# A linear-attention block with an MLP on one core: key sums in three groups, value weights loaded twice, a new order of the work ahead of the MLP

## The chip, the core and the metric

The kernel runs on one core of a Trainium2 chip. The core has five engines that work side by side, each through its own list of instructions in order: TensorE (PE, with its weight loads shown as PEld), VectorE (DVE), ScalarE (ACT), GpSimd (POOL) and SyncE (SP), which here only issues DMA transfers. Engines wait for each other through semaphores. The metric is the device time of one execution in microseconds (us).

## The reference

The input x has 2048 rows of 576 bf16 numbers. There are 32 heads of 18 numbers. Layer norms have no learned scale.

```
y        = layernorm(x)
q, k, v  = y @ wqkv                                  (each 2048 x 576, in 32 heads)
phi(t)   = [softmax(t @ w_phi), softmax(-t @ w_phi)]  per head, 36 features
kv, z    = sum over all rows of phi(k) v^T  and of phi(k)
o        = phi(q) kv / (phi(q) z + 1e-6)
h        = x + o @ wo
out      = h + gelu(layernorm(h) @ w1 + b1) @ w2 + b2  (hidden width 4608)
```

No query can be finished before the sums kv and z over all 2048 rows are there.

## The kernel before, in words

Rows are held in 16 tiles of 128, taken as eight pairs p = 0..7 with two tiles a = 0, 1 each; 576 columns are two halves i = 0, 1 of 288. All engines run a list that is written out by hand: the calls from line 771 on are the program order, and each engine takes its own instructions from it in that order.

Every function named here issues instructions for one engine (or the queue of one):

- Setup: `load_wk`, `load_x`, `load_values`, `load_wq`, `load_wo`, `load_w1`, `load_biases` are DMA issues on SP's queue (some slices of w1 on POOL's). `warm` runs products of an identity matrix on TensorE. `spread` (L217, POOL) lays w_phi out as blocks `bd`.
- Folding: `flip_mm` (L365) transposes the key weights on TensorE, `flip_ev` (L371) copies the result out, `fold_k_mm` (L381) multiplies them by the blocks, so that one product gives k @ w_phi; `fold_k_ev` (L389) copies to `wkp`. The query weights are turned by DMA (`turn_wq`, L374), folded by `fold_mm("q", c)` (L396), and `swap_q` copies row halves between partitions.
- Layer norm: `stats` (L293, L294, DVE), `power` (L300, L302, POOL: a variance to the power -1/2), `centre` (L266, POOL), `scale` (L272 on ACT or L314 on DVE). Then the tile is transposed: for pairs 0 and 1 on TensorE (`turn_x_mm`, `turn_x_ev`), for the others by DMA (`turn_dma`, L321).
- Projections: `key_mm`, `value_mm`, `query_mm` (all L426). A projection is 18 products of 64 rows each, for a = 0 on partitions 0-63 and a = 1 on 64-127, 288 columns wide. Weights must therefore stand in both halves of the partitions: `load_values` fills partitions 0-63 of `wv`, and `copy_values` (L174, POOL) copies to 64-127.
- After a projection: `key_exp`, `query_exp` (L448, ACT, two exponentials), `value_ev` (L436, ACT); `key_sum` (L477, L479, DVE) gives reciprocal sums; `key_weigh` (L483) multiplies by them, on POOL.
- `sums(p, a)` (L562): 11 products of full height (128 rows) that add one tile's phi(k) v^T to `acc_kv`. They need both halves i of the weighed features of that tile.
- The turn to the MLP: `table` (DVE) masks the sums, `combine_mm` (L648) multiplies the queries of tiles 0 and 1 by them, `divide` (L661, L662, DVE), `turn_o_mm`, `residual_mm` (L697), `residual_add` (L706), `residual_stats` (L714), `second` (L719, L254 and a root on POOL, L256), `rescale` (L260), `turn2_mm`, `turn2_ev` (L343). Query projections stand between these steps.
- The MLP: `up` (L1150, L1172) and `down` (L1194, L1198) for one, one, two, two, two pairs; the attention of later pairs (`norm_q`, `leave`, `enter`) is called from inside these loops.

PSUM results of the part ahead of the MLP rotate through three buffers (`two`, bufs=3), so a product waits until the result three steps before it has been copied out. Weighed keys rotate through five buffers (`exk_pool`). The weights of the first half of the setup borrow the memory of `w1_0`, and wkp, the turned queries of pair 0 and the MLP's input share `shared`.

## Time and profile before

| | us |
|---|---|
| median of 3 runs | 392.02 (391.94 to 392.32) |
| the profiled execution | 392.69 |
| its span, first to last instruction | 391.0 |
| first key projection starts | 15.82 |
| first combination of queries with the sums | 71.03 |
| MLP starts | 85.23 |
| first `down` starts | 103.15 |

The profile names engines as above, with the line of the kernel; "pk", "pv", "pW", "acc_kv", "pn", "pa", "ph" and "po" are the PSUM tiles of key and query projections, value projections, folds, key sums, combinations, residual, and the MLP's two products. In a row of the timeline or chain stand the start, the length and the number of instructions. The end of a product is modelled, so a product that waits in the pipeline can count as busy.

### The profile page before, as it was taken

Reading aid. Unit: us, or ns where it says so; the run is one execution under the profiler, and the core shown is the slowest. Engines: PE = TensorE matmul, PEld = TensorE weight load, DVE = VectorE, ACT = ScalarE, POOL = GpSimd, SP = SyncE. Lnnn points to the kernel's source line nnn. Section 1 sums busy time; section 2 is a strip of 40 time slices with the busy share of each in tenths; the row PEclk is TensorE's granted clock in tenths of the full one; section 3 lists DMA queues with packets and bytes.
Section 4 is the critical chain, followed back from the end, with each engine's and each line's share of the span. In section 5 each row is a group of like instructions: output and inputs, shape, how many; then the busy total and the mean of one; then the engine's idle time right before and its main releaser. Section 6 shows DMA issues by size and latency. Waiting matters only on the chain.

```text
span 391.0 us, 10251 instructions
## 1 busy us (share of the span) xinstructions
PE 383.6 (98%) x4492; PEld 267.2 (68%) x4493; DVE 163.5 (42%) x367; ACT 163.7 (42%) x290; POOL 128.2 (33%) x167
## 2 busy tenths in 40 slices
PE   8899999999999999999999999999999999999997
PEld 4687777779878887844457887444677764447773
DVE  6989894595249388590029322000480000000100
ACT  3978887678501850056650000666300026661000
POOL 8899999214604564144003111000031110000120
PEclk9999999999999999999999999999999999999999
DMA  8999749999655666643005542000041000000000
GB/s 220 189 182 175 163 98 184 227 300 254 206 106 104 95 107 134 107 61 62 0 2 63 90 106 48 16 1 2 2 102 50 17 17 0 2 2 0 17 29 18
DMA packets 76108, 34.76 MB, mean 89 GB/s; under 512 B 63026, under 2 KB 73536, under 8 KB 76064
## 3 DMA queue, kind: packets, MB, share of 16 engines
q1 hardware_dynamic: 75376, 32.47, 41.9%
q0 software_dynamic: 400, 1.35, 1.3%
q8 instruction: 35, 0.57, 0.6%
q10 hardware_dynamic: 288, 0.30, 0.3%
q14 instruction: 9, 0.07, 0.1%
HBM read 16.53 MB, written 2.36 MB: 48 GB/s over the span
## 4 chain that ended last, share of the span: by engine, by line
PE 94%; DVE 4%; POOL 1%; issue 1%; POOLq 0%
PE po L1194 36%; PE ph L1150 36%; PE pk L426 7%; PE pa L697 5%; PE pv L426 4%; PE acc_kv L562 2%; PE pw L250 1%; PE pn L648 1%; DVE st L293 1%; POOL wv L174 1%; DVE ob L662 0%; PE pW L396 0%; DVE shared L260 0%; PE pT L338 0%; DVE shared L314 0%
## 5 line engine op out<-in xcount | busy, mean ns | idle before, releaser
L1172 ACT ACTIVATE home<-ph,b1col 128x512 bf16<-128x512 f32 (+1 forms) x180 | 98.5, 598 | 169.6 <-PE ph L1150 166.3
L1194 PE MATMUL po<-w,home 128*128 128x288 bf16 (+2 forms) x1151 | 143.3, 286 | 0.1
L1150 PE MATMUL ph<-shared,w 64*128 64x512 bf16 (+2 forms) x1638 | 141.3, 332 | 0.1
L1194 PEld LDWEIGHTS <-home 128*128 128x128 bf16 x1152 | 109.2, 98 | 32.3 <-issue 1.8
L1150 PEld LDWEIGHTS <-w 64*128 64x128 bf16 x1638 | 80.3, 94 | 60.0 <-issue 1.0
L1198 DVE TENSOR_TENSOR ot<-po,hb 128x288 bf16<-128x288 f32 (+2 forms) x32 | 14.5, 454 | 106.5 <-PE po L1194 100.7
L1183 POOL TENSOR_TENSOR hb<-xh,b2bc 128x576 f32<-128x576 bf16 x16 | 20.4, 1272 | 104.6 <-DVE ot L1198 95.2
L426 PEld LDWEIGHTS <-home 64*128 64x128 bf16 x864 | 42.0, 94 | 10.8 <-issue 1.1
L512 POOL TENSOR_TENSOR padded<-home,rq 128x540 bf16<-128x540 bf16 x32 | 34.8, 1101 | 36.4 <-DVE rq L504 14.9
L256 POOL TENSOR_TENSOR rs<-va,mhalf 128x1 f32<-128x1 f32 x16 | 8.8, 550 | 105.0 <-DVE va L254 105.0
L706 DVE TENSOR_TENSOR xh<-pa,xh 128x288 bf16<-128x288 f32 x32 | 13.2, 449 | 71.6 <-PE pa L697 71.6
L483 POOL TENSOR_TENSOR phik<-phik,rk 128x576 bf16<-128x576 bf16 x32 | 36.4, 1164 | 1.4 <-PE pv L426 0.9
L477 DVE TENSOR_REDUCE sk<-phik 128x64 f32<-128x1152 bf16 x16 | 21.2, 1327 | 5.4 <-ACT phik L448 5.4
L448 ACT ACTIVATE home<-pk 128x576 bf16<-128x576 f32 x32 | 18.9, 649 | 6.9 <-PE pk L426 5.7
L503 DVE TENSOR_REDUCE sk<-home 128x64 f32<-128x1152 bf16 x16 | 21.0, 1313 | 0.0
L426 PE MATMUL pv<-wv,home 64*128 64x288 bf16 x288 | 20.9, 283 | 0.1
L426 PE MATMUL pk<-wqp,home 64*128 64x288 bf16 x288 | 20.0, 283 | 0.2 <-ACT home L448 0.2
L448 ACT ACTIVATE phik<-pk 128x576 bf16<-128x576 f32 x32 | 18.7, 652 | 3.1 <-PE pk L426 3.1
L426 PE MATMUL pk<-shared,home 64*128 64x288 bf16 x288 | 19.9, 283 | 0.0
L661 DVE RECIPROCAL rec<-pn 128x18 f32<-128x18 f32 (+1 forms) x32 | 8.0, 250 | 27.9 <-PE pn L648 27.9
L697 PE MATMUL pa<-wo,shared 64*128 64x288 bf16 x288 | 18.8, 283 | 0.0
L697 PEld LDWEIGHTS <-shared 64*128 64x128 bf16 x288 | 13.9, 94 | 4.3 <-issue 0.5
(78 smaller groups left out, 209.0 us busy)
## 6 DMA issues: line engine op xcount, KB each, us to landing
w<-in_B_w_dram SPq DMA_DIRECT2D x21, 432.0 KB, 7.0
out_dram<-ot SPq DMA_DIRECT2D x15, 144.0 KB, 1.9
xh<-in_A_x_dram SPq DMA_DIRECT2D x3, 576.0 KB, 7.3
wo<-in_A_wo_dram SPq DMA_DIRECT2D x4, 324.0 KB, 6.3
w<-in_B_w_dram POOLq DMA_DIRECT2D x3, 432.0 KB, 10.5
wv<-in_A_wqkv_dram SPq DMA_DIRECT2D x2, 324.0 KB, 9.9
w<-in_A_wqkv_dram SPq DMA_DIRECT2D x4, 157.5 KB, 8.7
wqp<-wqp SPq DMA_DIRECT2D x2, 288.0 KB, 3.9
```

Source lines behind the costliest of these rows:

```text
L426: nc.tensor.matmul(dst[:, a, 0:HALF], lhs[rows, c, :], w[rows, slot, i * HALF : (i + 1) * HALF], start=(n == 0), stop=(n == KC - 1),)
L448: nc.scalar.activation(rows[:, :, i * HH : (i + 1) * HH, s, :], flight[key, p, i][:, :, 0:HALF].rearrange("p a (h f) -> p a h f", f=DH), A ...
L477: nc.vector.tensor_reduce(sk[:, :, :], part_of(dst, i), AX.X, ALU.add)
L483: eng.tensor_tensor(part, part, flight["r" + key, p, i][:, a, :].rearrange("p (h o) -> p h o", o=1).to_broadcast([P, NH, DH]), ALU.mult,)
L503: nc.vector.tensor_reduce(sk[:, :, :], part_of(phiq[p], i), AX.X, ALU.add)
L512: eng.tensor_tensor(padded[:, a, g0 * P : (g0 + 5) * P].rearrange("p (g k) -> p g k", k=P)[:, :, 0:STEP].rearrange("p g (h f) -> p g h f", ...
L697: nc.tensor.matmul(pa[a], oT[p % 2][rows, c, :], wo[rows, c, cs], start=(c == 0), stop=(c == KC - 1),)
L1150: nc.tensor.matmul(ph[half][:, lo:hi], w1[p_ // 9][rows, c, p_ % 9 * P : (p_ % 9 + 1) * P], ln2T[rows, c, base + lo : base + hi], start=(c ...
L1172: nc.scalar.activation(hidden(m), ph[half][:, 0:width], AF.Gelu_apprx_tanh, bias=b1col[:, m : m + 1], scale=1.0,)
L1183: nc.gpsimd.tensor_tensor(hb[:, :], xh[:, t, :], b2bc[:, :], ALU.add)
L1194: nc.tensor.matmul(po[:, :], hidden(m)[:, i_ * P : (i_ + 1) * P], w2[m // 18][:, m % 18, cs], start=(j == 0), stop=(j == NM - 1),)
L1198: nc.vector.tensor_tensor(ot[:, cs], po[:, :], hb[:, cs], ALU.add)
```

## The change

- The key weights `wk` are loaded by row chunks (64, 256 and 256 rows of 576) and kept 640 wide with zeros; `flip_mm(c)` transposes one row chunk for all five head groups, and `flip_ev` copies 5 x 128 columns.
- The first key projection adds its nine chunks in the order in which they were folded.
- `load_values(e, half)` loads the value weights from DRAM into both halves of the partitions, in four loads of full rows; `copy_values` is gone.
- `load_wq(c)` loads one chunk per call, and the calls stand apart in the order; `load_wo(half)` takes nine rows of wo as one piece, with the columns of `divide`'s output ordered to match (runs of 2 instead of 18).
- `power(p)` serves one pair for p = 0..3, and two pairs in one call for p = 4 and 6 (the roots of 4 tiles).
- `ones` moves from POOL to DVE, the last slice of w_phi from POOL's DMA queue to ACT's, and three `key_weigh` calls from POOL to DVE. The masks of `window_masks` come later.
- `rescale(t)` writes one half of the doubled MLP input, `mirror(t, dve)` copies it to the other.
- `warm(12)` for `warm(13)`, and a new order for everything up to the MLP. The `sums` stand in three groups.

The helpers, cut:

```
-    def load_values(i):
-        nc.sync.dma_start(
-            wv[0:KH, :, i * HALF : (i + 1) * HALF],
...
-    def copy_values(i, part, copy):
-        cs = slice(i * HALF, (i + 1) * HALF)
-        ks = slice(part * 5, 5 + part * 4)
-        copy(wv[KH:P, ks, cs], wv[0:KH, ks, cs])
+    def load_values(e, half=0, eng=nc.sync):
+        c0, c1 = ((0, 5), (5, KC))[e]
+        eng.dma_start(
+            wv[half * KH : (half + 1) * KH, c0:c1, :],
+            A_wqkv[c0 * KH : c1 * KH, 2 * D : 3 * D].rearrange("(c k) f -> k c f", k=KH),
+        )
...
     def power(p):
...
+        n = 2 if p < 4 else 4
+        at = 2 * (p % 2)
+        va = small.tile([P, 4], FP32, name="va", tag="va")
+        nc.gpsimd.tensor_scalar(
+            va[:, 0:n], moments[p // 2][:, at : at + n, 1], 1.0, EPS, ALU.mult, ALU.add
+        )
+        rs = small.tile([P, 4], FP32, name="rs", tag="rs")
+        nc.gpsimd.tensor_tensor(rs[:, 0:n], va[:, 0:n], mhalf[:, 0:n], ALU.pow)
...
-    def flip_mm(g):
+    def flip_mm(c):
+        pX = flight["w", c] = two.tile([P, NG, P], BF16, name="pX", tag="two")
+        for g in range(NG):
             nc.tensor.transpose(
+                pX[:, g, :], wk[:, c, g * 126 : g * 126 + P], ident[:, :]
             )
...
-        features("k", wkp, p, i, PLAIN)
+        features("k", wkp, p, i, PLAIN if p or i else [(c, c) for c in fold_order])
...
+    def load_wo(half):
+        nc.sync.dma_start(
+            wo[half * KH : (half + 1) * KH, :, :],
+            A_wo.rearrange("(k c) f -> k c f", c=KC),
+        )
...
-                o[:, :, :, h0:h1],
-                pv[:, :, 0:DH].rearrange("p h (c e) -> p c e h", e=2),
+                o[:, :, h0:h1, :],
+                pv[:, :, 0:DH].rearrange("p h (e c) -> p c h e", e=2),
...
-    def rescale(t, half):
+    def rescale(t):
         mv, rs = moved[t]
-        normalise(ln2[t % 2][:, :, half, :], chunks(t), mv, rs, 0)
+        normalise(ln2[t % 2][:, :, 0, :], chunks(t), mv, rs, 0)
+
+    def mirror(t, copy):
+        copy(ln2[t % 2][:, :, 1, :], ln2[t % 2][:, :, 0, :])
```

The order that TensorE sees from the first key projection to the residual, before and after (k, v, q: a projection of pair and half; s: the key sums of pair and tile; f: a query fold):

```
before: k00 k01 v00 k10 v01 v11 k20 k21 v10 s00 v20 k11 v21 k30 v30 k31 s01 v31 f0 s20 s21
        f3 f2 v41 f1 k40 f4 k41 s10 s11 k50 k51 s31 v40 q00 v50 s41 s30 q01 q50 s40 v51 k60
        q30 k61 s51 v60 s50 v61 k70 k71 q70 v70 q40 s61 q71 v71 q20 s60 s70 s71 q60
        combine, q41 q31, transpose of o, q10 residual q61 residual q51 q11 q21
after:  k00 v01 v00 k10 v10 v11 k11 k01 k20 v20 k21 v21 k30 v30 v31 f1 s10 f2 s11 f3 s01 f0 f4
        s00 k31 k40 v40 k50 k51 k41 q00 v41 s20 s21 s31 s30 v51 v50 q01 q20 k60 v60 k61 q40 v70
        k70 v61 k71 q70 v71 q31 q30 q60 s50 s40 s41 s51 s61 s60 s70 s71 q50
        combine, q71 q51, transpose of o, q10 residual q41 residual q11 q21 q61
```

SP's queue up to the last turn of the query weights, before and after:

```
before: wk wk wk, x 2-3, x 4-7, values, values, x 8-11, wq (5 loads), turn of pair 2, wo, wq turn 4,
        wo, wq turn 1, turn of pair 3, wq turns 2, 3, 0, turn of pair 4, x 12-15, wo, ...
after:  wk wk wk, x 2-3, x 4-7, values (4 loads), x 8-11, wq 4, 2, 0, 1, wq turn 4, wq 3, turn of
        pair 2, x 12-15, wq turn 0, turn of pair 3, wq turns 3, 2, 1, biases, turns of pairs 4, 5, ...
```

More of the change, by code (lines that the diff above doesn't have):

```diff
@@ L585, with load_w1 @@
     w2 = []
-    def load_w1(q, n, eng):
+    def load_w1(q, n):
         c0, half = n // 2 * 3, n % 2
-        eng.dma_start(
+        (nc.gpsimd if q and half else nc.sync).dma_start(
             w1[q][half * KH : (half + 1) * KH, c0 : c0 + 3, :],
@@ L903 @@
     value_mm(3, 0)
-    key_weigh(2, 0, 0, pool)
-    value_ev(3, 0, act)
-    turn_wq(3)
-    turn_wq(0)
+    value_ev(3, 0, act)
+    key_weigh(1, 1, 0, pool)
+    key_weigh(0, 1, 1, pool)
+    value_mm(3, 1)
+    value_ev(3, 1, act)
+    key_weigh(1, 1, 1, pool)
+    fold_mm("q", 1)
+    fold_ev("q", 1, act)
+    load_biases()
+    sums(1, 0)
+    scale(5, 0, vec)
+    key_weigh(0, 1, 0, pool)
+    fold_mm("q", 2)
+    fold_ev("q", 2, act)
+    sums(1, 1)
+    key_sum(2, 0)
+    fold_mm("q", 3)
@@ L908 @@
+    sums(0, 1)
+    fold_ev("q", 3, act)
+    turn_dma(4)
+    scale(5, 1, vec)
+    key_weigh(2, 0, 1, pool)
+    turn_dma(5)
+    fold_mm("q", 0)
+    fold_ev("q", 0, act)
+    fold_mm("q", 4)
+    sums(0, 0)
+    key_sum(3, 0)
+    key_weigh(2, 0, 0, pool)
+    stats(6, 0)
+    swap_q(2)
+    key_weigh(3, 0, 1, pool)
+    key_weigh(3, 0, 0, pool)
+    fold_ev("q", 4, act)
+    swap_q(0)
+    key_sum(2, 1)
+    key_weigh(2, 1, 1, pool)
+    key_weigh(2, 1, 0, pool)
     key_mm(3, 1)
     key_exp(3, 1)
-    key_sum(1, 0)
@@ L979 @@
+    key_mm(5, 1)
+    key_exp(5, 1)
+    stats(6, 1)
     stats(7, 0)
     stats(7, 1)
-    sums(4, 1)
+    power(6)
+    centre(6, 1)
+    key_mm(4, 1)
+    centre(7, 0)
+    key_sum(4, 0)
+    swap_q(1)
+    query_mm(0, 0)
+    load_w1(0, 0)
+    value_mm(4, 1)
+    sums(2, 0)
+    load_wo(0)
+    key_exp(4, 1)
+    key_weigh(4, 0, 1, pool)
+    query_exp(0, 0)
+    scale(6, 1, act)
+    scale(6, 0, vec)
+    turn_dma(6)
+    scale(7, 0, act)
+    key_weigh(4, 0, 0, pool)
+    value_ev(4, 1, act)
@@ L1022 @@
[L1022 to L1027 removed]
+    turn_dma(7)
+    query_mm(0, 1)
+    query_mm(2, 0)
+    query_exp(0, 1)
+    query_exp(2, 0)
+    key_mm(6, 0)
+    key_exp(6, 0)
+    query_sum(0, 0)
+    query_weigh(0, 0, 0, pool)
+    value_mm(6, 0)
+    value_ev(6, 0, act)
+    key_mm(6, 1)
+    query_mm(4, 0)
+    value_mm(7, 0)
+    key_exp(6, 1)
+    query_exp(4, 0)
+    query_weigh(0, 0, 1, pool)
```

527 lines of the change are left out of this document (216 added, 311 removed).

## The prediction

> **What bounds the kernel now.** I read the busy shares first, then a table by stages, then the chain of work that ended last, and last the timeline of the head. The page's first line and five rows of the table by stages (stretch, length, busy time of PE, PEld, DVE, ACT and POOL, granted clock, DMA share, GB/s):
>
> ```profile
> PE 383.6 (98%) x4492; PEld 267.2 (68%) x4493; DVE 163.5 (42%) x367; ACT 163.7 (42%) x290; POOL 128.2 (33%) x167
> 6.94:15.82 8.88, 6.90 (x134) 5.58 (x133) 8.08 (x24) 7.84 (x14) 7.60 (x15) 1.00 1.13 234
> 15.82:20.78 4.96, 4.84 (x75) 3.79 (x74) 4.75 (x13) 4.43 (x8) 4.67 (x5) 1.00 0.96 145
> 20.78:71.03 50.25, 50.25 (x867) 39.17 (x866) 39.41 (x61) 40.51 (x69) 46.16 (x52) 1.00 0.91 164
> 71.03:85.23 14.20, 13.15 (x214) 10.15 (x212) 10.38 (x29) 10.12 (x18) 2.58 (x5) 1.00 1.05 258
> 85.23:391.00 305.77, 302.95 (x3195) 206.57 (x3196) 97.10 (x230) 99.33 (x182) 61.73 (x72) 1.00 0.30 61
> ```
>
> TensorE is the bound: from 20.78 to 71.03 it has no idle time. The MLP behind 85.23 is out of reach: the edits there touch DVE alone, which is busy 97 of 306 us. So the change can act on four things: the head before 15.82, TensorE's waits that a row counts as busy, the price of TensorE's changes between kinds of work, and the 1.05 us of idle time between 71.03 and 85.23. The chain shows the second and third:
>
> ```profile
> 16.84 1.38 POOL wv L174
> ...
> 19.35 1.39 POOL wv L174
> ...
> 20.78 2.36 PE pv L426 x35
> ...
> 25.35 1.10 PE pv L426 x18
> 26.45 0.41 PE acc_kv L562 x11
> 26.87 1.21 PE pv L426 x18
> ...
> 35.21 0.37 PE pW L396 x5
> 35.58 0.63 PE acc_kv L562 x22
> 36.21 0.54 PE pW L396 x10
> 36.74 1.21 PE pv L426 x18
> ...
> 68.84 1.04 PE acc_kv L562 x33
> 69.88 1.21 PE pk L426 x18
> ```
>
> A projection (18 products of 64 rows) costs 1.10 us, but 1.21 behind a full-height group (the key sums acc_kv or the folds pW). Eleven key-sum products cost 0.41 alone and 33 cost 1.04, so eleven more cost (1.04-0.41)/2 = 0.315. A visit to full-height work therefore costs 0.41-0.315 = 0.10 on the way in and 1.21-1.10 = 0.11 on the way out: 0.2 us, whatever it holds. Between 15.82 and 71.03 the chain has 13 such visits, the first at 26.45, the last at 68.84.
>
> **The sum for the stretch as it is.** 41 projections (16 key, 16 value, 9 query) at 1.103 are 45.2; 16 key sums at 0.315 are 5.0; five folds at 0.27 (ten products in 0.54) are 1.35; 13 visits are 2.6. That is 54.2, and the stretch has 71.03-15.82 = 55.2: 1.0 us is waiting hidden in busy rows. Part of it is seen in the head:
>
> ```profile
> 1.42 5.73 PE L250 MATMUL pw<-ident 128*128 128x512 bf16 x13 [1.42 <-POOL ident masks.py:199]
> 6.94 1.94 PE L365 MATMUL pX<-ident,w 128*128 128x128 bf16 x25
> 9.49 0.69 ACT L343 COPY home<-pT 128x640 bf16<-128x640 bf16 x1
> 10.11 5.06 ACT L389 CAST shared<-pW 128x576 bf16<-128x576 f32 x9
> 15.21 0.68 PE L338 MATMUL pT<-ident,shared 128*128 128x128 bf16 x9 [1.17 <-ACT shared L389]
> 15.82 2.38 PE L426 MATMUL pk<-shared,home 64*128 64x288 bf16 x36
> 18.04 1.50 PE L426 MATMUL pv<-wv,home 64*128 64x288 bf16 x18
> ```
>
> The value projection at 18.04 has 1.50 where two key projections have 2.38: it sits among POOL's copies of the value weights.
>
> **The change, part by part.**
>
> *Head, to the first key projection.* One warm-up product less (5.73/13 = 0.44) ends the warm-up at 6.5. The transposes of the key weights now go by row chunk and are copied 640 wide, four by ACT at 0.69, so ACT is through at 7.0+2.8 = 9.8; then the nine fold copies (5.06) and one turn copy of 0.69 before the ninth: 15.5. DVE has, from about 8.1 on (6.5 and four of five groups of transposes at 1.94/5), two copies, four tiles' statistics and four rescales to do before that; by the rows further down 0.42, 1.1 and 0.5 each, 7.4 in all, so it comes out level. So the first key projection starts at 15.5 instead of 15.82: -0.3. Bounds: the first transposes cannot start before the load (no earlier than now), 0; if the copies overlap as closely as the casts, -0.7.
>
> *POOL.* Off it go the four value copies, the ones (to DVE), three key weighings (to DVE) and two of eight root calls. TensorE gains only what waited for the copies. The ones come on DVE before the first key's reduction, and the first key sum on TensorE 15 projections (16.5 us) later, which covers them whatever they cost. A weighing on DVE costs between 0.5 (a rescale of the same elements) and 1.16 (POOL's own); I take 0.8, and three of them fit DVE's free 10.8 us between 20.78 and 71.03.
>
> *Key sums.* The new order holds them in three groups: four between the five query folds in one full-height block, four in one block after the value projection of pair 4, the last eight in one block. Three visits for 13: -10 x 0.2 = -2.0. Bounds: nothing, if TensorE waits inside the blocks for the weighings by as much; -2.1, if the folds also cost less.
>
> *Loads.* Rows for the queue (issue time, then issue to landing), the transfers' sizes from the page:
>
> ```profile
> L374 SPq DMA_TRANSPOSE w<-w x5: 1214/1253/1957, 20.0 to 28.2; - x5
> ...
> DMA to landing us min/median/max: 2.6/4.2/4.7
> L164 SPq DMA_DIRECT2D wv<-in_A_wqkv_dram x2: 705/867/1029, 3.6 to 4.4; - x2
> ...
> DMA to landing us min/median/max: 9.1/9.9/10.8
> ...
> wv<-in_A_wqkv_dram SPq DMA_DIRECT2D x2, 324.0 KB, 9.9
> ...
> xh<-in_A_x_dram SPq DMA_DIRECT2D x3, 576.0 KB, 7.3
> ...
> wo<-in_A_wo_dram SPq DMA_DIRECT2D x4, 324.0 KB, 6.3
> ```
>
> The second row half of the value weights is 648 KB more; the values landed at 4.4+10.8 = 15.2 and are now wanted at 15.5+1.1 = 16.6. The last turned piece of the query weights landed at 28.2+4.2 = 32.4, and the first query fold came at 35.21. In the new order that fold is reached after 15 projections: 15.5+16.5+0.1 = 32.1, and it takes the piece that is turned last. Before this turn stand 648 KB of values and the last 576 KB of x that came later before; 648 KB of output weights have gone behind it. [...] I take a landing at 32.5 to 33.3 and so waits of 1.2 us in all (values, pair 2's turn and this fold share them), against 1.0 before: +0.2. [...]
>
> *From the combination to the MLP.* The work is the same (seven query projections on TensorE); its end is set by DVE:
>
> ```profile
> 79.74 0.46 DVE L706 TENSOR_TENSOR xh<-pa,xh 128x288 bf16<-128x288 f32 x1 [0.40 <-PE pa L697]
> 80.23 0.46 DVE L714 BATCH_NORM_STATS2 st<-xh 128x6 f32<-128x288 bf16 x1
> 80.72 0.21 DVE L719 BATCH_NORM_AGGREGATE mv<-st 128x2 f32<-128x12 f32 x1
> 80.97 0.15 DVE L254 TENSOR_SCALAR va<-mv 128x1 f32<-128x1 f32 x1
> 82.37 2.01 DVE L260 TENSOR_SCALAR shared<-xh,mv,rs 128x576 bf16<-128x576 bf16 x4
> 84.31 1.67 DVE L343 COPY shared<-pT 128x512 bf16<-128x512 bf16 x4
> ```
>
> Two adds 0.92, two statistics 0.92, two aggregates 0.42, two variances 0.3, four rescales 2.0, two of the four copies 0.83: 5.4 of the 5.5 us from 79.74 to 85.23. Two of the rescales become copies of the same 576 elements; between nothing and 0.5 each, I take 0.4, nearer to the rescale: -0.2, and with the adds first the POOL root is covered, -0.1: -0.3 in all. The division has the same elements in runs of 2 instead of 18; I put it at nothing, with +1.8 (four of them doubled) as the far end.
>
> *All else* (roots for four tiles at once, output weights in two loads, biases earlier, a slice of the feature weights on ACT's queue) lies beside TensorE's work; the MLP's weights start when the last key sum ends and move with it.
>
> **Sum.** -0.3 -2.0 +0.2 -0.3 = -2.4 us. The profiled execution takes 392.69 (span 391.0), 0.7 above the median of 392.02; a difference made within the first holds for the second: 389.6.
>
> **The rivals.**
>
> *The weights come late (slower).* Place: the first query fold. For it: a saturated queue (DMA share 1.13 in the head), 576 KB more before the last turn, the fold 3 us earlier. [...] If the second value halves are not cheap and the 648 KB of output weights give nothing back, 1224 KB at 164 to 234 GB/s are 5.4 to 7.6 us: a landing at 37.8 to 40.0, where TensorE waits 5.7 to 7.9 us and 1.0 was waited before; with the -2.6 of the other terms 394.1 to 396.3, at the middle 395.2. It decides from a landing at 35.7 on (3.6 us of waiting). [...] Chance 0.17.
>
> *The last block waits for weighings.* POOL's weighings are the one thing that ended close before the last sums:
>
> ```profile
> 65.10 3.40 POOL L483 TENSOR_TENSOR phik<-phik,rk 128x576 bf16<-128x576 bf16 x3
> ...
> L483 POOL TENSOR_TENSOR phik<-phik,rk x32: 1159/1163/1171, 22.1 to 67.3; 128x576 bf16<-128x576 bf16 x32
> ```
>
> They end at 68.5. I have the new last one at about 65 (from 21.7 on 29 at 1.16 are 33.7, and POOL's other work in the stretch is 46.2 - 32 x 1.16 = 9.0) and the last two sums at 67 to 68. If POOL ends at 68.5 as now, the sums end at 69.1 and the combination starts at 70.4: -0.6 -0.3, 391.1. [...] No lengthening shows in the row: 32 weighings lie within 1159 and 1171 ns beside a busy DVE. Chance 0.09.
>
> *A visit is not what costs.* If what looks like the price of a change is paid in any order, only -0.3+0.2-0.3 are left: 391.6, within 0.2%. Against: 1.21 and 1.10 alternate exactly so. Chance 0.08.
>
> *More.* All waits go (-1.0 instead of +0.2) and the head gains 0.7: 392.0-0.7-2.0-1.0-0.4 = 387.9. Chance 0.12.
>
> **How the numbers follow.** The forecast, 388.4 to 391.0 around 389.6, has 0.54. Within 0.2% (0.8 us, about what the runs can tell apart) lies the fourth case's 0.08. Faster by more: 0.54, 0.12 and the 0.09, which ends just outside; slower 0.17. The range goes from 387.3, below the largest gain, to 392.8, into the late weights; this leaves out the rest of that rival and a little below, under 0.2.
>
> **What would show it.** Key sums in three groups on TensorE with 0.315 per eleven; the first key projection near 15.5; no POOL copy of wv; the first query fold without an idle line before it, or, if I am wrong, a wait of its weight load for the DMA that writes w; the combination at 69, the MLP at 82.5, and from there the same 306 us. A wait inside the last block for POOL, or a division that takes 0.9, would make the forecast wrong.

## The result: 0.9% slower, and the profile after

The changed kernel takes 395.62 us (median of five runs, 395.07 to 396.6) beside 392.13 (391.94 to 392.36) for the kernel before: a ratio of 1.0089, with a 95% interval of 1.0072 to 1.0105. The forecast was 389.6 with a range of 387.3 to 392.8. The profiled execution of the changed kernel took 396.6 (span 394.9), that of the kernel before 392.69 (391.0), so the two traces differ by 3.9.

The busy shares and the table by stages of the changed kernel (stretch, length, busy time of PE, PEld, DVE, ACT and POOL, granted clock, DMA share, GB/s). The stretches end at the first key projection, the first query fold, the last block of key sums, the combination and the MLP:

```profile
PE 381.9 (97%) x4491; PEld 265.2 (67%) x4492; DVE 169.0 (43%) x370; ACT 164.5 (42%) x292; POOL 116.6 (30%) x153
0.00:15.71 15.71, 11.12 (x146) 7.12 (x147) 10.94 (x34) 9.89 (x17) 8.47 (x29) 1.00 0.91 229
15.71:35.03 19.32, 16.99 (x273) 12.91 (x271) 16.24 (x34) 15.77 (x26) 11.18 (x16) 1.00 0.91 157
35.03:67.07 32.04, 32.04 (x566) 25.77 (x564) 30.19 (x39) 26.94 (x47) 28.89 (x31) 1.00 0.97 176
67.07:75.02 7.95, 5.40 (x109) 3.97 (x107) 5.13 (x9) 2.37 (x5) 4.66 (x5) 0.86 0.64 144
75.02:89.26 14.24, 13.41 (x215) 10.64 (x214) 9.94 (x29) 9.73 (x18) 1.51 (x3) 0.96 1.05 278
89.26:394.90 305.64, 302.95 (x3195) 204.78 (x3196) 96.52 (x230) 99.82 (x182) 61.86 (x72) 1.00 0.29 59
```

The first key projection starts 0.1 earlier than before, the 14.2 us from the combination to the MLP and the 305.6 behind it are what they were. All of the loss lies between 15.71 and 75.02: 59.3 us, where it was 55.2. TensorE is idle in both ends of this part, from 15.71 to 35.03 and from 67.07 to 75.02. The view of the waits, from 15 to 73 (engine and product, releaser, us in total, times, longest), and the chain of work that ended last say for what:

```profile
PE pk L423 <- DMA home<-shared: 2.3, 2, 1.6
PE acc_kv L559 <- POOL phik L480: 2.0, 2, 1.3
...
PE acc_kv L559 <- DVE phik L480: 0.6, 1, 0.6
```

```profile
22.08 3.26 DMA home<-shared
...
25.66 5.91 DMA home<-shared
...
60.10 5.13 DVE phik L480
65.23 1.27 DVE sk L474
...
69.18 3.10 POOL phik L480 x2
...
72.81 2.27 PE pk L423 x18
```

Three things are new. **In the head** two key projections wait for the turns of x, pair 2 (landed 22.08+3.26 = 25.35) and pair 3 (25.66+5.91 = 31.57): 0.86 and 1.8 from the end of the product before, 2.7 in all (the view counts 2.3, because the modelled end of that product reaches into the wait). **In the last block of key sums** TensorE waits for weighings, in three pieces of 0.7, 0.9 and 1.5, counted in the same way: the chain goes back from them to one weighing on DVE that took 5.1 to 5.2. **Behind that block** a query projection takes 2.27 instead of the 1.21 that it takes behind full-height work, at a granted clock of 0.50 (rows in experiment 4).

The sum over the stretch: -2.0 for the visits, -1.0 for the waits that were there before, +2.7, +3.1 and +1.1 give +3.9, against 59.3-55.2 = +4.1.

### The profile page after: what moved, and what is told of

Its sections match the earlier page's. It is cut to its first block, busy times and chain, and to the rows that moved or that the text cites. A ratio compares the mean times of both kernels' runs of the same rounds, so it can differ in the third digit from the quotient of the medians.

```text
span 394.9 us, 10223 instructions
## 1 busy us (share of the span) xinstructions
PE 381.9 (97%) x4491; PEld 265.2 (67%) x4492; DVE 169.0 (43%) x370; ACT 164.5 (42%) x292; POOL 116.6 (30%) x153
## 4 chain that ended last, share of the span: by engine, by line
PE 81%; DVE 9%; DMA 4%; POOL 2%; ACT 1%; issue 1%; POOLq 0%; DVEq 0%
PE po L1188 36%; PE ph L1144 36%; PE pa L691 5%; DVE sk L474 3%; DMA home<-shared 2%; PE pk L423 2%; DVE st L275 1%; PE pn L642 1%; DMA w<-in_A_w_phi_dram 1%; DVE phik L480 1%; DVE rk L476 1%; POOL phik L480 1%; DVE shared L310 1%; DVE sk L500 1%; POOL rs L288 1%
## 5 line engine op out<-in xcount | busy, mean ns | idle before, releaser
L1144 PEld LDWEIGHTS <-w 64*128 64x128 bf16 x1638 | 78.4, 94 | 62.1 <-issue 0.7
L480 POOL TENSOR_TENSOR phik<-phik,rk 128x576 bf16<-128x576 bf16 x29 | 33.7, 1194 | 10.5 <-DVE rk L476 10.5
L423 PE MATMUL pv<-wv,home 64*128 64x288 bf16 x288 | 19.6, 283 | 0.0
```

The lines of the kernel that those rows point to most:

```text
L423: nc.tensor.matmul(dst[:, a, 0 : hi - lo], lhs[rows, c, :], w[rows, slot, lo:hi], start=(n == 0), stop=(n == KC - 1),)
L480: eng.tensor_tensor(part, part, flight["r" + key, p, i][:, a, :].rearrange("p (h o) -> p h o", o=1).to_broadcast([P, NH, DH]), ALU.mult,)
L1144: nc.tensor.matmul(ph[half][:, lo:hi], w1[p_ // 9][rows, c, p_ % 9 * P : (p_ % 9 + 1) * P], ln2T[rows, c, base + lo : base + hi], start=(c ...
```

## The experiments

Each kernel was run beside the kernel before on the same chip; ratios are to that kernel, with 95% intervals. The changed kernel was not run again beside them; the median of the kernel before lies between 392.08 and 392.47 there, so a difference of some 0.4 us from the changed kernel says nothing. One more spread matters for single traces: the changed kernel and experiments 1 to 4 have the same head, and reach the first key projection between 15.00 and 16.27. A start later on is therefore best read from there.

**1. One weighing back to POOL.**

```
-    key_weigh(5, 1, 0, vec)
+    key_weigh(5, 1, 0, pool)
```

> One word is changed in the kernel after: the weighing of pair 5, tile 1, row half 0 goes from DVE back to POOL; the two other weighings on DVE stay. Theory A (that weighing, 5.2 us on DVE beside four weighings on POOL, made the last key sums late; the idle TensorE then lost its clock): POOL goes on without its idle 4.6 us and ends its weighings near 64.6 + 3 x 1.16 = 68.1, at most 0.5 later where one of DVE's two falls beside them; the last key sum ends near 69.2 instead of 72.8, the projection behind it takes 1.1 instead of 2.3, and the kernel 395.6 - 3.6 - 1.2 = 390.8, between 390.4 and 392. Rival B (POOL alone is the bound of the last block, whoever does that weighing): the weighing costs POOL 1.16 more and the kernel takes 395.6 or up to 396.8. Rival C (the weighing was slow by itself, by its shape or place): the two that stay on DVE are of the same shape and would be slow again where they have been 0.69 and 1.71.

Measured: 392.14 us, ratio 0.9986 [0.9971, 1.0002]; 3.5 us less than the changed kernel, for one word. The combination starts at 71.0 instead of 75.0; from the first key projection (15.00 here) it is 56.0 us instead of 59.3. The waits for weighings are gone from the list, and the projection behind the block takes 1.21. The weighings of this kernel (engine, tiles, count, shortest/median/longest in ns, first and last start):

```profile
L480 POOL TENSOR_TENSOR phik<-phik,rk x30: 1162/1166/1170, 24.4 to 66.9; 128x576 bf16<-128x576 bf16 x30
...
L480 DVE TENSOR_TENSOR phik<-phik,rk x2: 745/2266/3786, 64.9 to 68.6; 128x576 bf16<-128x576 bf16 x2
```

The same instruction takes 0.745 or 3.786 here, 0.693 to 5.215 in the changed kernel: so not its shape (rival C) but what runs beside it. And the two that stayed are still held up, only not where TensorE waits for them. Theory A holds on the cause; it had expected 390.8 and a range to 392.0, so the gain is smaller than its sum, and just outside its range.

**2. All three back to POOL.**

> In the kernel after all three weighings go from DVE back to POOL. Theory A (DVE and POOL hold each other up when both weigh): no weighing on POOL takes more than 1.17, where two took 1.46 and 1.67; POOL has five weighings left at 64.6 and ends near 64.6 + 5 x 1.165 = 70.4, the last key sum near 70.9; TensorE's wait is then about 1 us in more than one piece and the clock stays up: 395.6 - 1.9 - 1.2 = 392.5, between 391.5 and 394, which is slower than with one weighing given back. Rival B (three weighings on DVE cost nothing and POOL's total decides): slower than after by up to 3 x 1.16 = 3.5, up to 399.

Measured: 393.33 us, 1.0017 [1.0002, 1.0032]. No weighing on POOL takes more than 1.18, TensorE waits 0.7 for one, and the combination starts at 72.4 (56.2 behind the first key projection, which came at 16.27): 2.3 us faster than the changed kernel, 1.2 slower than with one given back. Rival B, by which more work on POOL could only cost, is out.

**3. What the two engines do to each other.** The timelines of the changed kernel on DVE and on POOL (start, length, engine, instruction, count, idle time before it and its releaser):

```profile
60.01 5.21 DVE L480 TENSOR_TENSOR phik<-phik,rk 128x576 bf16<-128x576 bf16 x1
65.15 1.34 DVE L474 TENSOR_REDUCE sk<-phik 128x64 f32<-128x1152 bf16 x1
...
59.81 0.32 POOL L519 TENSOR_TENSOR padded<-home,rq 128x72 bf16<-128x72 bf16 x1
60.08 4.53 POOL L480 TENSOR_TENSOR phik<-phik,rk 128x576 bf16<-128x576 bf16 x4
69.18 3.09 POOL L480 TENSOR_TENSOR phik<-phik,rk 128x576 bf16<-128x576 bf16 x2 [4.57 <-DVE rk L476]
```

DVE's weighing stands from 60.01, 0.2 after POOL began a short instruction (L519), and ends at 65.23, 0.62 after POOL's four weighings in a row have ended at 64.61. Behind it in DVE's order are the key sums of pair 7, whose factors POOL needs, so POOL then stands idle for 4.57, and TensorE for 3.1. In the weighing of experiment 1 that took 3.786 the same holds (POOL's run ends at 68.10, DVE's weighing at 68.71).

The kernel before has no such instruction on DVE beside POOL's weighings. Its costliest groups on DVE from 15 to 80 (line, engine, operation, tiles, count, busy time, mean ns, idle time before) read one tile each; the rescale takes its two factors for each row besides:

```profile
L477 DVE TENSOR_REDUCE sk<-phik 128x64 f32<-128x1152 bf16 x16 | 21.2, 1327 | 5.4 <-ACT phik L448 5.4
L479 DVE RECIPROCAL rk<-sk 128x64 f32<-128x64 f32 x16 | 8.8, 553 | 0.8
L293 DVE BATCH_NORM_STATS2 st<-xh 128x6 f32<-128x288 bf16 x18 | 7.0, 433 | 0.0
L314 DVE TENSOR_SCALAR shared<-xh,mv,rs 128x576 bf16<-128x576 bf16 x6 | 2.9, 490 | 0.0
```

To change the place of an operand, and not the work, the next kernel lets DVE read the factors from PSUM, where TensorE's results stand, instead of SBUF, where both operands of a weighing stood:

```
+    def set_apart(p, i, a):
+        n = 400 + 32 * len(apart)
+        apart[p, i, a] = acc_kv[:, 0, n : n + NH]
+        nc.vector.tensor_copy(apart[p, i, a], flight["rk", p, i][:, a, :])
...
-            flight["r" + key, p, i][:, a, :].rearrange("p (h o) -> p h o", o=1).to_broadcast(
+            apart.get((p, i, a), flight["r" + key, p, i][:, a, :]).rearrange("p (h o) -> p h o", o=1).to_broadcast(
...
     key_sum(5, 1)
+    set_apart(5, 1, 0)
...
     key_sum(7, 0)
+    set_apart(7, 0, 0)
...
+    key_sum(7, 1)
+    set_apart(7, 1, 1)
     sums(5, 0)
     sums(4, 0)
-    key_sum(7, 1)
```

> The kernel after, with its three weighings still on DVE, but each reads its 32 factors from a free part of the key sums' bank in PSUM, where DVE puts a copy of them right behind the key sum (three copies of 32 columns; the key sum of pair 7, half 1 is called for a few steps earlier, which leaves DVE's order but for the copies as it was). So each weighing has one operand in SBUF and one in PSUM. Theory A (two operands in SBUF make DVE wait for POOL's run of weighings, and POOL for DVE): no DVE weighing takes more than 1.2, none on POOL more than 1.18, POOL's idle 4.6 us behind 64.6 is gone, the last key sum ends near 69.7, the combination starts near 70.9 instead of 75.0, and the kernel takes 395.6 - 3.7 = 391.9, between 391.2 and 392.8. Rival B (DVE and POOL hold each other up wherever the factors are): a weighing of 3 to 5 us on DVE again, the kernel within 1 us of 395.6.

```profile
L487 POOL TENSOR_TENSOR phik<-phik,rk x29: 1162/1166/1171, 23.9 to 66.5; 128x576 bf16<-128x576 bf16 x29
...
L487 DVE TENSOR_TENSOR phik<-phik,acc_kv x3: 694/753/754, 60.4 to 70.6; 128x576 bf16<-128x576 bf16 x3
```

All three weighings take 0.69 to 0.75, and no weighing on POOL is lengthened. Only the first of them, at 60.44, lies beside POOL's weighings; in the last kernel below all three do (57.49, 60.36 and 63.30, 0.69 to 0.76), again without lengthening POOL's. That is theory A on the cause. The time is another matter: 394.41 us, 1.0057 [1.0038, 1.0077], where 391.9 was expected. The factors lie in the tile of the key sums, so DVE's last two weighings now wait 4.4 us for TensorE's key sums, and TensorE 1.7 for them, and the projection behind them takes 2.27 at half the clock again. The cause was removed and a dependence of my own put in its place; the last kernel below avoids it.

**4. The clock.** Nine products into a bank that nobody reads keep TensorE busy during the waits:

```
+    warm(3)
     sums(7, 0)
     key_weigh(7, 0, 1, pool)
     key_weigh(7, 1, 1, vec)
+    warm(6)
     sums(7, 1)
```

> Nine products into a bank that nobody reads are added in the kernel after: three ahead of the key sums of pair 7, tile 0, and six ahead of those of tile 1 (2 us of TensorE's 3.1 us of waiting there). The waits themselves stay. Theory A (the low granted clock at 72.7 to 76 comes from the idle TensorE just before): the last key sum ends at 72.8 as before, the projection behind it takes 1.1 to 1.3 instead of 2.3, the combination 0.7 instead of 1.1, and the kernel 395.6 - 1.5 = 394.1. Rival B (the clock falls there for another reason): the projection takes 2.3 again and the time is the same or up to 0.5 longer.

Measured: 395.37 us, 1.0064 [1.0042, 1.0087], 0.3 less than the changed kernel by the medians and 0.25% less by the ratios, whose intervals overlap: the runs do not tell the two apart. The profiled execution cannot decide either, because in it the first weighing on DVE got in and the waits are gone: the same instructions up to 60 us, but another winner.

```profile
60.23 0.72 DVE L480 TENSOR_TENSOR phik<-phik,rk 128x576 bf16<-128x576 bf16 x1
...
60.02 0.31 POOL L519 TENSOR_TENSOR padded<-home,rq 128x72 bf16<-128x72 bf16 x1
60.28 8.32 POOL L480 TENSOR_TENSOR phik<-phik,rk 128x576 bf16<-128x576 bf16 x6
```

So the outcome can differ between executions. The clock differs too, and its record in the traces shows a pattern. In the changed kernel's trace the record starts with the full clock at 4.46 us; the clock falls to half at 72.73, 20 times 3.413 us later, and stays there for 3.41. In the traces of experiments 3 and 7 and of the second kernel of experiment 10 it falls 19 times 3.413 us after the start of the record, again for 3.41. Tables in these lengths, for the changed kernel and then for experiment 5 (the turns first, below), both with more than 3 us of waiting in this block:

```profile
69.31:72.73 3.42, 1.05 (x22) 0.80 (x22) 1.94 (x2) 0.13 (x1) 2.96 (x2) 1.00 0.64 136
72.73:76.14 3.41, 3.41 (x44) 2.29 (x40) 1.16 (x5) 1.02 (x2) 1.95 (x3) 0.50 0.50 125
76.14:79.55 3.41, 3.13 (x50) 2.29 (x49) 2.50 (x9) 2.25 (x5) 0.00 (x0) 1.00 1.05 226
```

```profile
65.81:69.23 3.42, 1.87 (x60) 1.64 (x56) 3.32 (x5) 1.87 (x4) 1.19 (x1) 1.00 1.09 262
69.23:72.64 3.41, 1.79 (x35) 1.40 (x35) 1.81 (x5) 0.00 (x0) 2.24 (x3) 1.00 0.24 52
72.64:76.05 3.41, 3.27 (x62) 2.36 (x58) 2.53 (x9) 2.39 (x5) 1.61 (x3) 1.00 0.86 188
```

In the changed kernel the waits fall into one of these lengths, in which TensorE works 1.05 of 3.42, and the next is granted half the clock. In experiment 5 they lie in two of them, 1.87 and 1.79 of work are left, and the clock stays at 1.00. The other three traces with a fall have 1.20, 1.77 and 1.72 of work in the length ahead of the half clock; the third kernel of experiment 10 has 1.60 and no fall, so no limit can be read from the work in one length.

So in the four traces with a fall the low clock comes behind the waiting, as theory A has it, but waits as long were followed by none in experiment 5. That it depends on how the waits lie in these lengths is my reading, and the 1.60 speaks against it; what decides is not shown. Executions with a lower mean clock are 3 of 5 for the changed kernel and 7 of 9, 5 of 6 and 4 of 5 in experiments 5, 7 and 8, which keep these waits, and 1 of 12 in experiment 1, which does not (a mean does not say where in the run the clock fell). The two of the changed kernel that kept theirs took 395.07 and 395.25, so the clock is a small part of its loss. The kernel before has lower clocks as well: of its executions beside experiments 1, 2, 4 and 5, the 21 with a mean clock of 0.999 or more have a median of 392.28, the seven with 0.991 to 0.996 one of 393.62.

**5. The turns first.** Only SP's order is changed:

```
-    turn_wq(4)
     scale(2, 0, act)
+    turn_dma(2)
+    turn_wq(4)
...
-    turn_dma(2)
...
-    load_x(12, 16)
-    turn_wq(0)
...
     turn_dma(3)
+    turn_wq(0)
+    load_x(12, 16)
```

> Only SP's order is changed in the kernel after: the turn of pair 2 is issued ahead of the first turn of the query weights, and the turn of pair 3 ahead of the load of the last x and the second turn of the query weights. Theory A (SP works in order, so those two turns waited behind a turn that waited for its load): the turn of pair 2 lands near 21.8 as before the change, that of pair 3 near 27 to 28, TensorE's two waits of 0.86 and 1.8 for them are gone; TensorE reaches the first query fold near 32.4 instead of 35.0, and the piece of the query weights that this fold takes is turned last and still lands near 34, so 1 to 1.7 of the 2.7 come back there. With POOL, DVE and the last block as they are, the kernel takes 395.6 - 1.0 = 394.6, between 393 and 395.6. Rival B (the transfers are late because the queues are full, whatever the order): the turns land no earlier, and the time is the same within 0.5.

Measured: 395.32 us, 1.0067 [1.0045, 1.0089]. The two waits for turns are gone. In their place, as foreseen:

```profile
PE pW L393 <- DMA w<-w: 1.1, 1, 1.1
```

The waits in the last block stay (2.0 for POOL, 1.2 for DVE), which leaves 0.3 of the median, less than was expected and inside the spread of its runs (392.88 to 397.04).

**6. The value loads alone**, in the kernel before:

```
-    def load_values(i):
+    def load_values(i, half=0):
...
-            wv[0:KH, :, i * HALF : (i + 1) * HALF],
+            wv[half * KH : (half + 1) * KH, :, i * HALF : (i + 1) * HALF],
...
     load_values(0)
+    load_values(0, 1)
     load_values(1)
+    load_values(1, 1)
...
-    copy_values(0, 1, gps)
-    copy_values(1, 1, gps)
-    copy_values(0, 0, gps)
-    copy_values(1, 0, gps)
```

> The kernel before, with nothing but its value weights loaded as in the change: each of the two loads has a twin that fills rows 64 to 127, right behind it on SP, and POOL's four copies are gone. Theory A (the prediction's small term: POOL is relieved, the loads cost little): the value projections in the head no longer stand among copies, and the kernel takes 391.7 to 392.3. Rival B (648 KB more ahead of x 8 to 11 and the query weights, at 234 GB/s 2.8 us later for all that stands behind them): the values land near 18, the first value projection waits up to 1 us, the turns of pair 2 and of the query weights come later, and the kernel takes 393 to 395.

Measured: 395.42 us, 1.0073 [1.0059, 1.0088]. This part by itself costs 3.0 us. One wait and two issues on SP tell how:

```profile
PE pk L426 <- DMA home<-shared: 2.9, 1, 2.9
```

```profile
7.18 3.47 SPq L179 DMA_DIRECT2D xh<-in_A_x_dram  x1
19.42 1.44 SPq L321 DMA_TRANSPOSE home<-shared  x1
```

The queue backs up: the issue of x 8 to 11 behind the values takes 3.47 where it took 1.1 before. The turn of pair 2 is issued at 19.42 instead of 17.68 (SP is through with the issues ahead of it at 19.3, and ACT with the work that the turn waits for at about the same time), and lands 6.0 after its issue instead of 4.1: 3.6 later in all. The values themselves are in time (16.6); what stands behind them is late.

**7. The twin loads taken out of the changed kernel**, with SP's order left as it is and POOL copying rows 64 to 127:

```
-    load_values(0, 1, nc.sync)
-    load_values(1, 1, nc.sync)
...
     power(1)
+    copy_values(0, 1)
+    copy_values(1, 1)
...
     power(2)
+    copy_values(0, 0)
+    copy_values(1, 0)
```

> The kernel after, with one of its parts undone: rows 64 to 127 of the value weights are copied by POOL again (four copies; the window masks go behind them), and the 648 KB of twin loads are gone. The three weighings on DVE stay, so the last block is as uneven as before. Read from the head: theory A (the 648 KB put off everything that SP issued behind them): the first piece of the query weights lands near 16.3 instead of 19.1, its turn is issued near 16.5 instead of 19.2, the turn of pair 2 lands near 22.5 instead of 25.35 and that of pair 3 near 28.5 to 29 instead of 31.57, and no projection waits over 0.5 for a turn. Rival B (SP's order alone made the turns late): they land within 1 us of where they were and the waits of 0.86 and 1.8 stay. In time: a value projection that waits up to 2 us for the copies takes back much of what the turns give; 394.5 to 395.5 with A, 396 to 397 with B.

SP's timeline of the changed kernel, and then of this one:

```profile
19.20 2.15 SPq L368 DMA_TRANSPOSE w<-w  x1
...
22.08 1.54 SPq L317 DMA_TRANSPOSE home<-shared  x1
...
25.66 2.26 SPq L317 DMA_TRANSPOSE home<-shared  x1
```

```profile
15.10 1.54 SPq L373 DMA_TRANSPOSE w<-w  x1
...
19.25 1.29 SPq L322 DMA_TRANSPOSE home<-shared  x1
...
24.54 1.24 SPq L322 DMA_TRANSPOSE home<-shared  x1
```

The first turn of the query weights is issued 4.1 earlier, because its load lands at 14.95 instead of 19.12; the turn of pair 2 lands 2.8 after its issue, at 22.05 instead of 25.35. That of pair 3 is issued at 24.54 instead of 25.66; the trace has no landing for it, but the key projection that needs it starts at 30.27 without a wait, where in the changed kernel it landed at 31.57. No projection waits for a turn. Theory A: the bytes made them late. SP's order decided who paid: the turn of pair 2 stood behind a turn whose load was among the late ones. In time 395.67, 1.0101 [1.0064, 1.0137], just above the 394.5 to 395.5 of theory A: a key projection now waits 1.7 for ACT while POOL copies, and the last block waits and loses its clock as before.

**8. The ones back on POOL, and the first key sum earlier on DVE.**

```
-        nc.vector.memset(vals[:, :, :, DH], 1.0)
+        nc.gpsimd.memset(vals[:, :, :, DH], 1.0)
...
     centre(2, 0)
+    ones()
...
-    stats(4, 0)
-    ones()
-    stats(4, 1)
     centre(3, 1)
     key_sum(0, 0)
+    stats(4, 0)
+    stats(4, 1)
```

> The kernel after, with the ones column written by POOL again, ahead of its work for pair 3, and with the first key sum on DVE ahead of the statistics of pair 4; nothing else is changed, the three weighings stay on DVE with both operands in SBUF. Theory A (the ones on DVE, 1.75 of no visible work and 0.49 of memset, and the wait for x 8 to 11 ahead of the first key sum put off POOL's first weighing from 20.4 to 24.6, and POOL's run of weighings late in the stretch is what DVE's weighing then has to wait for): POOL's first weighing starts near 20.4, POOL is up to 4 us ahead of the queue and gets gaps, DVE's weighing gets in, the wait in the last block shrinks from 3.1 to under 1, and the kernel takes 392 to 393.5. Rival B (the prediction: the ones are covered whatever they cost): 395.6, within 0.7.

Measured: 396.33 us, 1.0093 [1.0077, 1.011]: my theory fell. POOL's first weighing starts at 19.4 instead of 24.6, as meant, and DVE's weighing at 59.42 takes 5.219 again, beside four on POOL that start 0.07 later, behind a short one that started 0.19 earlier. POOL's lead is used up long before it matters. The ones on DVE are covered, as the prediction had it, though they cost 2.2 there (1.75 without visible work and 0.49).

**9. Visits alone**, in the kernel before: six of the 13 visits joined to others.

```
-    sums(0, 0)
...
-    sums(0, 1)
...
+    sums(0, 0)
+    sums(0, 1)
     sums(2, 0)
...
-    sums(3, 1)
...
+    sums(3, 1)
     sums(4, 1)
...
-    sums(4, 0)
...
-    sums(5, 1)
...
+    sums(4, 0)
+    sums(5, 1)
     sums(5, 0)
...
-    sums(6, 1)
...
+    sums(6, 1)
     sums(6, 0)
```

> The kernel before, with nothing but its key sums moved on TensorE: those of pair 0 go to the ones of pair 2, tile 0; pair 3, tile 1 to pair 4, tile 1; pair 4, tile 0 and pair 5, tile 1 to pair 5, tile 0; pair 6, tile 1 to pair 6, tile 0. That leaves 7 visits to full-height work of 13. Theory A (a visit costs 0.2, the reading of the prediction): 6 x 0.2 = 1.2 less, 392.1 - 1.2 = 390.9, between 390.6 and 391.3, and the projections that no longer stand behind a visit take 1.10 instead of 1.21. Rival B (the price of a change is paid in any order, or comes back as a wait): 392.1, within 0.3.

Measured: 391.81 us, 0.9989 [0.9972, 1.0006]. In the profiled execution the combination starts at 69.11 instead of 71.03; 0.65 of that is the head, which came earlier (15.17 instead of 15.82) though nothing in it was changed. From the first key projection to the combination it is 53.94 instead of 55.21: 1.27 less, where 1.2 was expected, and projections that no longer stand behind a visit take 1.10. The medians differ by only 0.6, half of what was expected, and the interval reaches to no change; among executions with a mean clock of 0.999 or more the medians are 391.40 (8) and 392.41 (23). So the traces bear out the size, and the times agree in sign without settling it.

**10. All repairs together.** The first attempt joined the turns first (experiment 5), the ones on POOL (8), all weighings on POOL (2), and the folds in the order in which their pieces are turned:

```
-    fold_mm("q", 1)
+    fold_mm("q", 0)
...
-    fold_mm("q", 2)
+    fold_mm("q", 3)
...
-    fold_mm("q", 3)
+    fold_mm("q", 2)
...
-    fold_mm("q", 0)
+    fold_mm("q", 1)
...
     fold_mm("q", 4)
```

> The kernel after with four repairs: the turns of pairs 2 and 3 early on SP (as in the run with the turns first), the query folds in the order in which their pieces are turned (0, 3, 2, 1, 4), the ones written by POOL again, ahead of its work for pair 3, with the first key sum on DVE ahead of the statistics of pair 4, and all weighings on POOL. Theory A (what the change lost is made of these: late turns, POOL's late start, weighings on two engines): POOL's first weighing starts near 20.4 instead of 24.6, no projection waits for a turn, POOL's last weighing ends near 66.5, the combination starts near 68.5, and the kernel takes 392.1 - 0.1 - 2.0 - 1.0 = 389.0, between 388.7 and 390.5: faster than before by 0.8% and than after by 1.7%. Rival B (POOL's total decides wherever it starts, or another load is late): POOL ends at 68.5 or later and the kernel takes 391 to 393.

Measured: 393.32, 1.0014 [0.9996, 1.0032], within 390.99 to 397.09. The turn of pair 4 came late now (1.8). The second has three weighings on DVE again, with the edit of experiment 3:

> The same repairs of SP, of the folds and of the ones, with the three weighings on DVE with their factors in PSUM. If POOL is what ends last with all weighings on it, this is the faster of the two by up to 1 us; if TensorE is, the two are equal within 0.3. If DVE's weighings still wait for POOL, this one is slower, 391 or more.

Measured: 395.18, 1.0061 [1.0038, 1.0085], for the dependence of experiment 3 (TensorE waits 1.7 for it) and a turn that comes 2.3 late. The third puts the weighings ahead of the last block, the biases behind the turns of pairs 4 and 5, and one turn of the query weights ahead of that of pair 3:

```
     value_ev(1, 0, act)
+    turn_wq(0)
     scale(3, 0, act)
...
     turn_dma(3)
-    turn_wq(0)
...
-    load_biases()
...
     turn_dma(5)
+    load_biases()
...
     set_apart(7, 0, 0)
+    key_weigh(7, 0, 0, vec)
...
     set_apart(7, 1, 1)
+    key_weigh(7, 1, 1, vec)
...
-    key_weigh(7, 0, 0, vec)
...
-    key_weigh(7, 1, 1, vec)
```

> The combined kernel again, with what its traces showed: the first query-weight turn but one is issued ahead of the turn of pair 3 (SP stood idle for 1.0 there), the biases go behind the turns of pairs 4 and 5, and DVE's three weighings, with their factors in PSUM, come right behind their key sums, ahead of the last block of key sums. Expected: the turn of pair 4 lands by 36 and the wait of 1.8 for it is at most 0.5; POOL's last weighing ends near 66.5, the last key sum at 67.3, the combination starts near 68.4, and the kernel takes 390.1, between 389.3 and 391.5. If a wait for DVE at the start of the last block, or POOL, takes the place of what is gone, 391 to 392.5.

Measured: 392.62, 1.0 [0.9983, 1.0017]. Its combination starts at 67.3, the earliest of all (52.5 behind the first key projection), and then the chain of work has this line in the middle of a projection:

```profile
68.96 1.97 issue
```

Seven of its twelve executions ran at a lower mean clock (median 393.11, beside 390.91 for the other five). The fourth issues two loads earlier:

```
+    load_w1(0, 4)
+    load_wo(1)
     turn_q(0)
...
-    load_w1(0, 4)
-    load_wo(1)
```

> The last combined kernel, with two loads moved on SP: the last part of the first half of the MLP's first weights and the second half of the output weights are issued ahead of the two transposes of the first query features, where SP stood idle from 53.2 to 57.5, instead of behind them. In the kernel without this move TensorE had nothing to execute from 68.96 to 70.94, with no wait that the profile names, while 3 MB of loads were queued. Theory A (its instructions came late behind those loads): the gap of 1.97 is gone or under 0.5, the combination starts near 67.4 as there, and the kernel takes 390.4 - 2.0 = 388.5 where the clock stays up, between 388 and 390.5. Rival B (the gap has another cause): the gap stays, and the kernel takes 390.4 to 392.6 as without the move.

Measured: 391.41, 0.9989 [0.9973, 1.0004]. The gap is 0.67 and has moved to 64.4, into the last block, but the two loads now hold up the two transposes behind them: the second lands at 70.0 instead of 63.6, and the combination waits 1.4 for it (the 67.35 in the next expectation is the landing of the first). The fifth keeps only the first of the two there:

```
     load_w1(0, 4)
-    load_wo(1)
     turn_q(0)
+    load_wo(1)
```

> The last combined kernel with the output weights' second half behind the two transposes of the first query features again, and only the last part of the MLP's first weights ahead of them. There the transposes landed at 67.35, where 63.59 had been enough, and the combination waited 1.4 for them; 0.67 more was a gap without a wait that the profile names. Expected: the transposes land by 66, the combination starts near 68.4, and the kernel takes 391.4 - 1.4 = 390.0 with the gap and 389.3 without, between 389 and 391. If the gap without a named wait grows to the 2 us that it had two kernels ago, 391 to 392.

Measured: **389.07 us** (388.94 to 389.49), **0.9921 [0.9907, 0.9935]**. It beats the kernel before by 0.8% and the changed one by 1.7%, with no low clock in any of its five executions. Its table by stages, and its weighings on DVE and POOL side by side:

```profile
15.52:32.16 16.64, 16.64 (x272) 13.12 (x270) 15.73 (x33) 15.28 (x26) 13.14 (x17) 1.00 1.05 171
32.16:64.20 32.04, 32.04 (x565) 25.76 (x564) 30.01 (x46) 26.93 (x47) 30.14 (x32) 1.00 1.00 184
64.20:68.03 3.83, 3.83 (x108) 3.38 (x107) 1.05 (x4) 2.38 (x5) 1.80 (x3) 1.00 1.24 277
68.03:82.03 14.00, 12.99 (x214) 10.27 (x213) 10.02 (x29) 9.81 (x18) 2.57 (x5) 1.00 1.01 253
```

```profile
57.49 0.69 DVE L487 TENSOR_TENSOR phik<-phik,acc_kv 128x576 bf16<-128x576 bf16 x1
...
57.20 4.54 POOL L487 TENSOR_TENSOR phik<-phik,rk 128x576 bf16<-128x576 bf16 x4
```

From 15.52 to 68.03 TensorE has no idle time, and 0.69 on DVE beside four weighings on POOL stands where the changed kernel had 5.21. This kernel differs from the changed one in more than the two causes, in the order of the folds, the ones and the loads among others, so it shows that the waits can go, not what each repair is worth.

## Why the prediction was wrong, by its own steps

- **Head, -0.3.** The first key projection came at 15.71, not 15.5: -0.1. That shows nothing either way: identical heads reach it between 15.00 and 16.27 after the change, and at 15.17 and 15.82 before it.
- **POOL: "A weighing on DVE costs between 0.5 ... and 1.16 ...; I take 0.8, and three of them fit DVE's free 10.8 us".** This is the step that failed most. The shortest took 0.69 and 0.75, as bounded; beside POOL's four weighings one took 5.2, and with it went 3.1 us of TensorE, and in some executions its clock. Both ends of the bound were prices of an instruction by itself, and DVE's free 10.8 us did not show that it would stand for 5.2 beside POOL.
- **The rival of the last block.** It named the right place, and set against it a row: 32 weighings within 1159 to 1171 ns "beside a busy DVE". That row could not bear on the change: none of DVE's instructions beside those weighings reads two tiles from SBUF (rows in experiment 3). The weighing on DVE does: with both operands in SBUF it took up to 5.2 beside POOL's, and with one of them in PSUM 0.69 to 0.76 (experiments 3 and 10). I had only POOL ending late, and priced it at 1.5 (391.1 after 389.6); what decided was DVE held up, and POOL then waiting 4.57 for DVE's next key sums. On who waits: POOL was 0.2 into the short instruction at 59.81 when DVE's weighing came, and DVE then stood through four more instructions, each of which POOL started while DVE's was already there.
- **Key sums, -2.0.** Right in the traces: three groups, 0.315 to 0.32 for eleven products, and 1.27 for six visits in experiment 9; the run times alone do not settle the size. In the last kernel, where nothing waits, the stretch from the first key projection to the combination takes 52.5; the prediction's own terms give 54.2-2.0 = 52.2.
- **Loads, +0.2.** The second step that failed, mis-sized: 2.7 of waits in place of 1.0, so +1.7, and 3.0 for the loads alone (experiment 6). No run shows the landing at 32.5 to 33.3 and the 1.2 of waits that the +0.2 was made of. By the byte, 648 KB at the 164 and 234 GB/s of two stretches of the kernel before are 4.0 and 2.8 us, an estimate; the 3.0 of experiment 6 lies between. The waits came at the turns of x (0.86 for pair 2, which the term had named, and 1.8 for pair 3), not at the first query fold (35.03, without a wait), where the rival of the late weights put them.
- **Combination to the MLP, -0.3.** 14.24 after 14.20 in the changed kernel, where the combination still ran at the low clock; 14.00 in the last one: -0.2. The division costs what it did (0.42 and 0.50 for each call), as taken.
- **The MLP** takes 305.64 after 305.77: unchanged, as said.

Added up: -0.1 (head) -2.0 (visits) +1.7 (waits in the head, 2.7 for 1.0) +3.1 (last block) +1.1 (its clock) -0.1 (MLP) = +3.7, of the 3.9 between the two traces.

So the forecast of 389.6 is about what the change is worth with its late turns mended and its weighings kept apart: 389.07. That the two numbers come so close is in part luck: the last kernel has no wait left in the stretch where the forecast had allowed for 1.2, and it moves more than these two things. As it was made, a weighing on the wrong engine and 648 KB more where the DMA share was 0.91 to 1.13 already took back more than it gave.

## What to carry to other kernels

The same weighing took 0.69 or 5.21 on DVE here, by what POOL did beside it: price work that moves to an engine with free time beside what runs there at that moment, not by the instruction alone; and a row that shows no conflict counts only if the conflicting instruction was in it. The 648 KB put in where the DMA share was 0.91 to 1.13 already were paid here by what was issued behind them (the turn of pair 2 landed 3.6 later in experiment 6), so follow the next transfers that somebody waits for, not the one that was added. With one operand moved to PSUM the weighings of the two engines ran side by side here (0.69 to 0.76 on DVE, at most 1.17 on POOL), once the tile that it was put in brought no wait of its own.

## What was not expected of the hardware

- A DVE instruction with two SBUF operands waited through four POOL weighings in a row and ended 0.61 to 0.62 after the last; in another execution of nearly the same stream it went first and took 0.72, and POOL's next took 1.69 instead of 1.16. What decides stays open: in both it started while POOL was in a short instruction, 0.20 and 0.21 after that one's start.
- A gap of 1.97 in the middle of a projection, with no wait that the profile names ("issue"), while the loads for the MLP were queued. It shrank to 0.67 and then went away when loads were issued elsewhere; that its own instructions came late behind them is argued, not shown.
- More than 3 us of waiting in three pieces cost TensorE half its clock for 3.41 us in one execution (the changed kernel) and nothing in another (experiment 5). In the lengths of 3.413 us of experiment 4, 1.05 of work was left in one in the first and 1.87 and 1.79 in two in the second; since 1.60 in the third kernel of experiment 10 cost nothing and 1.77 in another trace came ahead of half the clock, what decides stays open.
